# First transfers of an attention and MLP kernel in the order of their use, and a third group of queries, keys and values asked for earlier

## The chip, the cores and the metric

The kernel runs on one core of one Trainium2 chip. The metric is the device time of one execution in microseconds (us); lower is better. Engines are named as the profile names them: PE (TensorE, matrix products), DVE (VectorE), ACT (ScalarE), POOL (GpSimd), and SP (SyncE, which here only issues transfers).

## The reference, cut to what matters

```python
def _attn_ref(q, k, v) -> np.ndarray:          # q, k, v: (4, 8, 576, 64)
    window = 128
    scale = 1.0 / np.sqrt(D)
    scores = scale * np.matmul(q, k.transpose(0, 1, 3, 2))
    rel = pos[:, None] - pos[None, :]
    slopes = 2.0 ** (-8.0 * (np.arange(H, dtype=np.float32) + 1) / H)
    bias = slopes[:, None, None] * (-np.abs(rel).astype(np.float32))[None, :, :]
    mask = (rel >= 0) & (rel < window)
    scores = np.where(mask, scores + bias[None], -1000000000.0)
    scores = scores - np.max(scores, axis=-1, keepdims=True)
    attn = np.exp(scores)
    attn = attn / (np.sum(attn, axis=-1, keepdims=True) + 1e-09)
    return np.matmul(attn, v).astype(np.float32)
...
    x = attn_out.transpose(0, 2, 1, 3).reshape(B * S, H * D)     # 2304 x 512
    h = x @ w_in;  g = np.maximum(0.01 * h, h);  x = g @ w_out    # 512 -> 2048 -> 512
    h = x @ w_in2; g = h * (1.0 / (1.0 + np.exp(-1.702 * h))); out = g @ w_out2
```

Windowed attention with a linear bias per head, over four batches of eight heads, and then two MLP layers over all 2304 rows. Queries and keys are drawn with a larger spread than the values.

## The kernel before, in words

**Tiling.** A group n is four heads of one batch (two pairs of heads), so there are eight groups. `steps` holds 32 attention steps of 128 queries or so, four for each group. Steps 0 to 7 are batch 0, its groups 0 and 1 in turn; from step 8 on a group's four steps follow one another. The third group (n = 2) is thus used first by step 8. The keys of a group lie in `kbuf`, a part of the big tile `y` that also takes the result of the layers (`ys`); queries and values lie in pool buffers of two each, tags "q" and "v".

**A step.** `att_scores(s)` (L247) makes scores of queries by keys on PE. DVE adds the bias and takes the maximum (`att_ttr`, L265), ACT the exponential and its sum (`att_exp`, L277), DVE the reciprocal (`att_rcp`), POOL the division (`att_norm`). Two steps later PE transposes (`att_trans`, L296), ACT or DVE copy the result out of PSUM (`att_evac`, L304 and L306, tile `pt`), and three steps later PE multiplies by the values (`att_av`, L331, tile `O`). ACT and DVE split that into a high and a low part in `x` (L347, L127), since the layers take three passes over such parts.

**Weights.** A weight block comes as raw words (`load_w`, tile `raw`, two buffers) and `conv_w` makes its high and low part: ACT L142, DVE L143, L145, L147, L150 and L151, POOL L153, ACT L154, and a subtraction on POOL (L127). These nine operations are spread over thirteen ticks in the attention part, and in this part work in scratch `cearly`, eight regions of `y`. A raw buffer is free after L151, so that the load of conversion x + 2 waits for L151 of conversion x. `convs` is the table of steps at which conversions begin; each emits the load after next. From step 8 on a group of matmuls of the first layer (`mm1`, L367; `mm2`, L404) is put behind each step.

**Order.** All engines work through their instructions in the order written. SP issues nearly all loads in one queue, ACT some of the first. Both queues use eight semaphores for their transfers in turn, so that an issue also waits till the transfer eight before it has landed. `load_first` issues the loads of the first two groups and of two raw blocks; `load_qk(2, ...)` is called in step 6 and `load_v(2)` in step 9; the later groups are asked for at their predecessor's steps with i = 1 and i = 3.

Of the kernel before, what the change touches and what calls it, by code (L numbers as in the profile page):

```python
# [7 lines left out]
F32 = mybir.dt.float32  # L8
F32R = mybir.dt.float32r
U32 = mybir.dt.uint32  # L10
# [4 lines left out]
B, H, S, D = 4, 8, 576, 64  # L15
# [9 lines left out]
NKB = S // 64  # L25
# [6 lines left out]
def attention_mlp_kernel(  # L32
        ctx: ExitStack, tc: tile.TileContext, qin, kin, v, w1i, w1o, w2i, w2o, out):
    nc = tc.nc
# [5 lines left out]
    def sb(shape, dt, tag, bufs):  # L40
        return pool.tile(shape, dt, tag=tag, name=tag, bufs=bufs)
# [5 lines left out]
    window = [True]  # L47
# [3 lines left out]
    def after(d, fn):  # L51
        later.setdefault(step[0] + d, []).append(fn)

    def tick():
        step[0] += 1
        for fn in later.pop(step[0], []):
# [13 lines left out]
    ys = const.tile([128, NT * 4], F32, name="y")  # L70
# [5 lines left out]
    kbuf = ys[:, NT * 4 - 4 * S:].rearrange("p (n a s) -> p n a s", n=2, a=2)  # L76
    stile.append(ys[:, NT * 4 - 4 * S - 12 * 64:NT * 4 - 4 * S].rearrange(
        "p (n c h k) -> p n c h k", n=2, c=3, h=2))


    cearly = [[ys[:, x:x + 512].bitcast(U32) for x in (1536 + 1024 * n, 2048 + 1024 * n)]
              for n in range(4)] * 2

    def emit_consts():
        tmp = stile[2].rearrange("p n c h k -> p (n c h k)")
        rel, far = tmp[:, 0:KW], tmp[:, KW:2 * KW]
# [29 lines left out]
    def load_w(n, p):  # L116
        layer, f = divmod(n, NF)
        raw = sb([128, 1024], U32, "raw", 2)
        nc.sync.dma_start(out=raw, in_=wsrc[layer][p][f].bitcast(U32))
        wraw[n, p] = raw  # L120

    def alloc_w(n):
        wt[n] = wt[n - 2 * CB] if n >= 2 * CB else sb(
            [128, 4, 512], F32R, "wA" if n < CB else "wB", CB)

    def sub(e, out, in0, in1):
        e.tensor_tensor(out=out, in0=in0, in1=in1, op=ALU.subtract)  # L127

    def conv_w(n, p):
        raw = wraw.pop((n, p)).rearrange("p (n two) -> p n two", two=2)  # L130
        lo32, hi32 = raw[:, :, 0], raw[:, :, 1]
        if window[0]:
            a, b = cearly[4 * p + n]
        else:
            a = sb([128, 512], U32, "ca", 2)
            b = sb([128, 512], U32, "cb", 1)
        af, bf = a.bitcast(F32), b.bitcast(F32)
        hi, lo = wt[n][:, 2 * p], wt[n][:, 2 * p + 1]
        early = window[0]
        at = (0, 2, 3, 4, 5, 6, 7, 10, 12) if early else range(9)  # L140
        ops = [
            lambda: nc.scalar.activation(af, hi32.bitcast(F32), AF.Abs),  # L142
            lambda: nc.vector.tensor_scalar(  # L143
                af, af, F32_MIN_EXP, F32_MAX_EXP, op0=ALU.max, op1=ALU.min),
            lambda: nc.vector.tensor_scalar(  # L145
                a, a, 0x07FFFFFF, 3, op0=ALU.bitwise_and, op1=ALU.logical_shift_left),
            lambda: nc.vector.scalar_tensor_tensor(  # L147
                out=a, in0=hi32, scalar=0xC0000000, in1=a,
                op0=ALU.bitwise_and, op1=ALU.bitwise_or),
            lambda: nc.vector.tensor_scalar(b, a, 0xFF800000, None, op0=ALU.bitwise_and),  # L150
            lambda: nc.vector.scalar_tensor_tensor(  # L151
                out=bf, in0=lo32, scalar=2.0 ** -52, in1=bf, op0=ALU.mult, op1=ALU.mult),
            lambda: nc.gpsimd.tensor_tensor(out=af, in0=af, in1=bf, op=ALU.add),  # L153
            lambda: nc.scalar.activation(hi, af, AF.Copy),  # L154
            lambda: (sub(nc.gpsimd if early else nc.vector, lo, af, hi.bitcast(F32)),
                     ready.add((n, p))),
        ]
        for d, fn in zip(at, ops):
            after(d, fn) if d else fn()
# [9 lines left out]

    qkv, values = {}, {}  # L170

    def rows(src, offset, dims):
        return bass.AP(tensor=src.tensor, offset=src.offset + offset, ap=dims)


    def load_part(e, n, a, lo, hi):
        b, g = divmod(n, 2)
        qq, kk = qkv[b, g]
        src = qin[b, 2 * g + a]
        for h in range(2):  # L180
            d = slice(64 * h, 64 * h + 64)
            e.dma_start(  # L182
                out=qq[d, a, 64 * lo:64 * hi].rearrange("p (m q) -> p m q", q=64),
                in_=src[d].rearrange("p (m h q) -> p m h q", h=2, q=64)[:, lo:hi, h])
        e.dma_start(
            out=kk[:, a, 64 * lo:64 * hi], in_=kin[b, 2 * g + a, :, 64 * lo:64 * hi])

    def load_qk(n, parts=((0, NKB),)):
        b, g = divmod(n, 2)
        qkv[b, g] = sb([128, 2, S], F32, "q", 2), kbuf[:, n % 2]  # L190
        for lo, hi in parts:
            for a in range(2):
                load_part(nc.sync, n, a, lo, hi)

    def load_v(n, e=None):
        b, g = divmod(n, 2)
        vv = sb([128, 2, NKB, 64], F32, "v", 2)
        values[b, g] = vv

        for a in range(2):  # L200
            for h in range(2):
                for r in range(2):
                    src = v[b, 2 * g + a, 64 * r:64 * r + 64, 0:NQB - r, 64 * h:64 * h + 64]
                    k0 = 64 * (h ^ a)
                    (e or nc.sync).dma_start(out=vv[k0:k0 + 64, a, r::2], in_=src)  # L205

    def load_first():
        for n in range(2):  # L210
            qkv[0, n] = sb([128, 2, S], F32, "q", 2), kbuf[:, n]
        for n in range(2):
            for a, e in enumerate((nc.sync, nc.scalar)):
                load_part(e, n, a, 0, 4)
        load_w(*wload.pop())
        for a, e in enumerate((nc.sync, nc.scalar)):
            load_part(e, 0, a, 4, NKB)
        load_w(*wload.pop())
        load_v(0)
        for a in range(2):  # L220
            load_part(nc.sync, 1, a, 4, NKB)
        load_v(1)

    sp, sm, pp, pt, ot = {}, {}, {}, {}, {}
# [266 lines left out]
    wload = [(n, p) for p in range(2) for n in range(2 * CB)]  # L491
# [25 lines left out]
    for _ in range(6):  # L517
        nc.tensor.matmul(
            out=wp[:, 0:256], lhsT=wz[:, 0:128], rhs=wz[:, 128:384], start=True, stop=True)
    load_first()  # L520
    emit_consts()
    for n in range(2 * CB):
        alloc_w(n)
    convs = (0, 2, 3, 5, 6, 8, 10, 12)
    nconv, credit = 0, 0.0
    with tc.manual_schedule():
        for s in range(NS + 3):
            tick()
            todo, half = [], 0
            if s < NS:  # L530
                b, g, i = steps[s]
                nxt = 2 * b + g + 1 if b else 2 * B
                if nxt < 2 * B and i == 1:
                    load_qk(nxt)
                att_scores(s)
                if s == 6:
                    load_qk(2, ((0, 4), (4, NKB)))
                todo = items(s)
                half = len(todo) // 2
            if s >= 3:  # L540
                att_av(s - 3)
            if s < NS and nxt < 2 * B and i == 3:
                load_v(nxt)
            if s == 9:
                load_v(2)
            tr = 2 <= s < NS + 2
            if tr:
                for n in range(2):
                    att_trans(s - 2, n)
            for x, p in todo[:half]:  # L550
                att_ttr(s, x, p)
            if 1 <= s <= NS:
                att_rcp(s - 1)
                for x, p in items(s - 1):
                    att_norm(s - 1, x, p)
            for x, p in todo[:half]:
                att_exp(s, x, p)
            tick()
            if s >= 3:
                att_hi(s - 3)  # L560
            if tr:
                att_evac(s - 2, 0, nc.scalar)
            for x, p in todo[half:]:
                att_ttr(s, x, p)
            if tr:
                att_evac(s - 2, 1, nc.scalar if s < 9 else nc.vector)
            tick()
            for x, p in todo[half:]:
                att_exp(s, x, p)
            if s >= 3:  # L570
                att_lo(s - 3)
            tick()
            if s in convs:
                conv_w(*wconv[nconv])
                nconv += 1
                if nconv < 4 * CB - 1:
                    load_w(*wload.pop())
            seen = S * ((s - 2) // 8) if s != 8 and s != 9 else TT
            credit += 1
            while credit >= 1:  # L580
                j, fn, x = groups[-1]
                layer, c, t = rounds[j]
                need = [(layer * NF + c * CB + f, int(fn is mm2)) for f in range(CB)]
                if not ready.issuperset(need) or fn is mm1 and (t + 1) * TT > seen:
                    credit = 0
                    break
                credit -= 1
                run_group()
                tick()
        window[0] = False  # L590
        steady(wconv[4 * CB:])
# [47 lines left out]
```

## Time and profile before

| | us |
|---|---|
| three runs | 938.66, 938.48, 939.23; median 938.66 |
| profiled execution | 939.52 |
| its span | 937.5 |
| PE busy in the span | 903.6 (96%) |
| DVE, POOL, ACT busy in the span | 561.8, 390.7, 385.8 |

Busy times are those of the profiled execution. A matmul's end is modelled, so PE's busy share doesn't say how near to its peak it is. The span leaves out what lies around the program, 2.0 us here. "PEclk" is the granted clock of PE, 1.00 being its full 2.4 GHz and 0.50 half of it. The timeline's first number is the start in us from the span's begin, the second the time of the group of instructions.

### The profile page before, as it was taken

The page shows a single profiled execution, that of the slowest core. Times are in us where ns is not written, and L with a number is a line of the kernel's source. Part 1 is how long each engine was busy: PE and PEld are TensorE (multiplying, and loading weights), DVE is VectorE, ACT ScalarE, POOL GpSimd, SP SyncE. Part 2 cuts the span into 40 slices and gives each one's busy share as a digit, 9 for nine tenths or more (in the row PEclk, how much of TensorE's full clock was granted, in tenths as well). Part 3 has the DMA queues.
Part 4 walks back from the last instruction along what each step waited for, and adds up shares of the span by engine and source line. Part 5 has one row for each costly group of instructions (what it writes and reads, how often), then busy time and mean ns, then how long its engine had stood idle before and what let it go on. Part 6 is the DMA issues. An engine that isn't in the chain of part 4 may idle for free.

```text
span 937.5 us, 16388 instructions
## 1 busy us (share of the span) xinstructions
PE 903.6 (96%) x6252; PEld 844.6 (90%) x6252; DVE 561.8 (60%) x1220; ACT 385.8 (41%) x970; POOL 390.7 (42%) x448
## 2 busy tenths in 40 slices
PE   5678999999999999999999999999999999999997
PEld 3567998999999999999999998989989899898986
DVE  4876776137856473828375754657584848576343
ACT  3856887344423232323245455333232323233221
POOL 3765554224434242424349743433242423333221
PEclk7887999999999999999999999999999999999999
DMA  6363641002202020202011110202020201110034
GB/s 176 94 181 94 140 101 58 1 23 68 91 23 69 10 81 1 68 23 69 23 45 46 46 46 23 68 23 68 1 68 23 68 23 45 45 45 1 1 90 113
DMA packets 53934, 53.49 MB, mean 57 GB/s; under 512 B 40544, under 2 KB 42080, under 8 KB 53856
## 3 DMA queue, kind: packets, MB, share of 16 engines
q1 hardware_dynamic: 51664, 51.59, 19.4%
q10 hardware_dynamic: 2192, 0.85, 0.4%
q8 instruction: 50, 0.82, 0.4%
q14 instruction: 28, 0.23, 0.1%
HBM read 47.71 MB, written 4.72 MB: 56 GB/s over the span
## 4 chain that ended last, share of the span: by engine, by line
PE 92%; DMA 3%; SPq 2%; ACT 1%; DVE 1%; issue 1%; ACTq 0%; DVEq 0%
PE pt L367 20%; PE S L367 20%; PE mm L413 14%; PE mm L404 11%; PE O L404 10%; PE O L413 7%; PE O L331 2%; PE pt L296 2%; PE mm L367 2%; PE S L247 2%; DMA y<-k 1%; SPq L205 1%; DMA q<-q 1%; SPq L182 1%; ACT st L277 1%
## 5 line engine op out<-in xcount | busy, mean ns | idle before, releaser
L127 POOL TENSOR_TENSOR g<-u,g 128x384 fp32r<-128x384 f32 x192 | 202.1, 1053 | 437.4 <-ACT g L388 303.6
L388 ACT ACTIVATE g<-u 128x384 fp32r<-128x384 f32 x192 | 100.3, 522 | 47.3 <-DVE u L382 44.2
L424 DVE TENSOR_TENSOR y<-y,mm 128x384 f32<-128x384 f32 x88 | 48.5, 552 | 109.5 <-PE mm L404 80.1
L367 PE MATMUL pt<-x,wB 128*128 128x384 f32 x552 | 104.3, 337 | 0.0
L367 PE MATMUL pt<-x,wA 128*128 128x384 f32 x540 | 102.1, 337 | 0.0
L367 PE MATMUL S<-x,wA 128*128 128x384 f32 x540 | 101.9, 336 | 0.0
L367 PE MATMUL S<-x,wB 128*128 128x384 f32 x540 | 101.9, 336 | 0.0
L367 PEld LDWEIGHTS pt<-x,wB 128*128 128x128 f32 x552 | 97.9, 188 | 2.0
L367 PEld LDWEIGHTS S<-x,wB 128*128 128x128 f32 x540 | 95.5, 188 | 2.2
L367 PEld LDWEIGHTS S<-x,wA 128*128 128x128 f32 x540 | 95.5, 188 | 2.1
L367 PEld LDWEIGHTS pt<-x,wA 128*128 128x128 f32 x540 | 95.8, 188 | 1.8
L153 POOL TENSOR_TENSOR ca<-ca,cb 128x512 f32<-128x512 f32 x56 | 78.0, 1393 | 37.4 <-DVE cb L151 35.3
L378 ACT ACTIVATE u<-S 128x384 f32<-128x384 f32 x48 | 23.5, 490 | 132.6 <-PE S L367 132.6
L413 PE MATMUL mm<-wA,g 128*128 128x512 f32 x288 | 74.8, 395 | 0.0
L413 PE MATMUL mm<-wB,g 128*128 128x512 f32 x288 | 74.7, 395 | 0.0
L382 DVE SCALAR_TENSOR_TENSOR u<-u,pt 128x384 f32<-128x384 f32 x48 | 26.6, 554 | 70.7 <-ACT u L378 70.7
L429 DVE SCALAR_TENSOR_TENSOR y<-mm,y 128x512 f32<-128x512 f32 x84 | 57.8, 689 | 11.5 <-PE mm L413 11.5
L382 DVE SCALAR_TENSOR_TENSOR u<-u,S 128x384 f32<-128x384 f32 x48 | 26.6, 555 | 62.6 <-ACT u L378 62.6
L376 ACT ACTIVATE u<-S 128x384 f32<-128x384 f32 x42 | 20.6, 491 | 105.7 <-PE S L367 105.7
L404 PE MATMUL mm<-g,wA 128*128 128x384 f32 x312 | 64.0, 340 | 0.0
L404 PE MATMUL mm<-g,wB 128*128 128x384 f32 x312 | 63.6, 339 | 0.0
L413 PEld LDWEIGHTS mm<-wB,g 128*128 128x128 f32 x288 | 53.4, 188 | 9.2
(92 smaller groups left out, 1585.5 us busy)
## 6 DMA issues: line engine op xcount, KB each, us to landing
raw<-w1i SPq DMA_DIRECT2D x16, 512.0 KB, 3.6
raw<-w1o SPq DMA_DIRECT2D x16, 512.0 KB, 3.5
raw<-w2i SPq DMA_DIRECT2D x16, 512.0 KB, 3.5
raw<-w2o SPq DMA_DIRECT2D x16, 512.0 KB, 3.4
out<-y SPq DMA_DIRECT2D x36, 128.0 KB, 2.4
q<-q SPq DMA_DIRECT2D x20, 144.0 KB, 4.6
y<-k SPq DMA_DIRECT2D x10, 288.0 KB, 5.1
v<-v SPq DMA_DIRECT2D x32, 80.0 KB, 2.5
```

What stands on the lines that cost most here:

```text
L127: e.tensor_tensor(out=out, in0=in0, in1=in1, op=ALU.subtract)
L153: lambda: nc.gpsimd.tensor_tensor(out=af, in0=af, in1=bf, op=ALU.add),
L247: nc.tensor.matmul(out=sp[s][bank][64 * u:64 * u + 64, col:col + 64 * w], lhsT=qq[d, a, 64 * m:64 * m + 64], rhs=kk[d, a, k1 - 64 * w:k1], ...
L367: nc.tensor.matmul(out=h, lhsT=w[:, a, k * 128:(k + 1) * 128], rhs=xs[:, b2, k, t0:t0 + TT], start=(m == 0), stop=(m == len(ops) - 1),)
L376: nc.scalar.activation(u, h, AF.Prelu, alpha=0.01)
L378: nc.scalar.activation(u, h, AF.Tanh, scale=0.851)
L382: nc.vector.scalar_tensor_tensor(out=u, in0=u, scalar=1.0, in1=h, op0=ALU.add, op1=ALU.mult)
L388: nc.scalar.activation(g[:, 0], u, AF.Copy)
L404: nc.tensor.matmul(out=yp, lhsT=wt[n0 + f][:, 2 + a, e * 128:(e + 1) * 128], rhs=gt[r, f][:, b2, :], start=(m == 0), stop=(m == len(ops) - 1),
L413: nc.tensor.matmul(out=y, lhsT=gt[r, f][:, b2, e * 128:(e + 1) * 128], rhs=wt[n0 + f][:, 2 + a, :], start=(m == 0), stop=(m == len(ops) - 1),)
L424: nc.vector.tensor_tensor(out=acc, in0=acc, in1=y, op=ALU.add)
L429: nc.vector.scalar_tensor_tensor(out=acc, in0=y, scalar=0.5, in1=acc, op0=ALU.mult, op1=ALU.add)
```

## The change

Four things are changed.

- `load_first` issues in another order. `load_part` is split into `load_q` (queries of one pair) and `load_k` (the keys of both pairs in one transfer). The first raw block now stands behind the keys 4 to 8 of the first group, the second behind those of the second group. Four query transfers of the first group move from SP's queue to ACT's, and ACT issues no keys any more.
- The third group is asked for at step 4 (queries and keys) and step 5 (values), and lies in its own part of `y`, `late`. The groups behind it use the pool buffers as before.
- Conversions in the attention part no longer have eight scratch regions. They take the pool tiles `ca` (two buffers) and `cb` (one), of which every third `ca` and every second `cb` are replaced by a region of `y`.
- `convs` changes from (0, 2, 3, 5, 6, 8, 10, 12) to (0, 2, 4, 5, 7, 8, 10, 11).

```diff
--- before.py
+++ after.py
@@ -76,10 +76,6 @@
     kbuf = ys[:, NT * 4 - 4 * S:].rearrange("p (n a s) -> p n a s", n=2, a=2)
     stile.append(ys[:, NT * 4 - 4 * S - 12 * 64:NT * 4 - 4 * S].rearrange(
         "p (n c h k) -> p n c h k", n=2, c=3, h=2))
-
-
-    cearly = [[ys[:, x:x + 512].bitcast(U32) for x in (1536 + 1024 * n, 2048 + 1024 * n)]
-              for n in range(4)] * 2
     def emit_consts():
         tmp = stile[2].rearrange("p n c h k -> p (n c h k)")
@@ -129,11 +125,9 @@
     def conv_w(n, p):
         raw = wraw.pop((n, p)).rearrange("p (n two) -> p n two", two=2)
         lo32, hi32 = raw[:, :, 0], raw[:, :, 1]
-        if window[0]:
-            a, b = cearly[4 * p + n]
-        else:
-            a = sb([128, 512], U32, "ca", 2)
-            b = sb([128, 512], U32, "cb", 1)
+        x = 4 * p + n if window[0] else 0
+        a = ys[:, 1536:2048].bitcast(U32) if x % 3 == 2 else sb([128, 512], U32, "ca", 2)
+        b = ys[:, 2048:2560].bitcast(U32) if x % 2 == 1 else sb([128, 512], U32, "cb", 1)
         af, bf = a.bitcast(F32), b.bitcast(F32)
         hi, lo = wt[n][:, 2 * p], wt[n][:, 2 * p + 1]
         early = window[0]
@@ -169,32 +163,39 @@
     qkv, values = {}, {}
-    def rows(src, offset, dims):
-        return bass.AP(tensor=src.tensor, offset=src.offset + offset, ap=dims)
-
-
-    def load_part(e, n, a, lo, hi):
+
+    late = ys[:, 2560:2560 + 6 * S].rearrange("p (n a s) -> p n a s", n=3, a=2)
+
+    def new_qk(n):
+        qkv[divmod(n, 2)] = ((late[:, 0], late[:, 1]) if n == 2 else
+                             (sb([128, 2, S], F32, "q", 2), kbuf[:, n % 2]))
+
+
+    def load_q(e, n, a, lo, hi):
         b, g = divmod(n, 2)
-        qq, kk = qkv[b, g]
-        src = qin[b, 2 * g + a]
         for h in range(2):
             d = slice(64 * h, 64 * h + 64)
+            src = qin[b, 2 * g + a, d].rearrange("p (m h q) -> p m h q", h=2, q=64)
             e.dma_start(
-                out=qq[d, a, 64 * lo:64 * hi].rearrange("p (m q) -> p m q", q=64),
-                in_=src[d].rearrange("p (m h q) -> p m h q", h=2, q=64)[:, lo:hi, h])
-        e.dma_start(
-            out=kk[:, a, 64 * lo:64 * hi], in_=kin[b, 2 * g + a, :, 64 * lo:64 * hi])
-
-    def load_qk(n, parts=((0, NKB),)):
+                out=qkv[b, g][0][d, a, 64 * lo:64 * hi].rearrange("p (m q) -> p m q", q=64),
+                in_=src[:, lo:hi, h])
+
+    def load_k(n, lo, hi):
         b, g = divmod(n, 2)
-        qkv[b, g] = sb([128, 2, S], F32, "q", 2), kbuf[:, n % 2]
-        for lo, hi in parts:
-            for a in range(2):
-                load_part(nc.sync, n, a, lo, hi)
-
-    def load_v(n, e=None):
+        nc.sync.dma_start(
+            out=qkv[b, g][1][:, :, 64 * lo:64 * hi],
+            in_=kin[b, 2 * g:2 * g + 2, :, 64 * lo:64 * hi].rearrange("a p s -> p a s"))
+
+    def load_qk(n):
+        new_qk(n)
+        for a in range(2):
+            load_q(nc.sync, n, a, 0, NKB)
+        load_k(n, 0, NKB)
+
+    def load_v(n):
         b, g = divmod(n, 2)
-        vv = sb([128, 2, NKB, 64], F32, "v", 2)
+        vv = (late[:, 2].rearrange("p a (n d) -> p a n d", d=64) if n == 2 else
+              sb([128, 2, NKB, 64], F32, "v", 2))
         values[b, g] = vv
         for a in range(2):
@@ -202,23 +203,28 @@
                 for r in range(2):
                     src = v[b, 2 * g + a, 64 * r:64 * r + 64, 0:NQB - r, 64 * h:64 * h + 64]
                     k0 = 64 * (h ^ a)
-                    (e or nc.sync).dma_start(out=vv[k0:k0 + 64, a, r::2], in_=src)
+                    nc.sync.dma_start(out=vv[k0:k0 + 64, a, r::2], in_=src)
     def load_first():
         for n in range(2):
-            qkv[0, n] = sb([128, 2, S], F32, "q", 2), kbuf[:, n]
-        for n in range(2):
-            for a, e in enumerate((nc.sync, nc.scalar)):
-                load_part(e, n, a, 0, 4)
-        load_w(*wload.pop())
-        for a, e in enumerate((nc.sync, nc.scalar)):
-            load_part(e, 0, a, 4, NKB)
+            new_qk(n)
+        load_q(nc.sync, 0, 0, 0, 4)
+        load_q(nc.scalar, 0, 1, 0, 4)
+        load_k(0, 0, 4)
+        load_q(nc.scalar, 1, 0, 0, 4)
+        load_q(nc.sync, 1, 1, 0, 4)
+        load_k(1, 0, 4)
+        for a in range(2):
+            load_q(nc.scalar, 0, a, 4, NKB)
+        load_k(0, 4, NKB)
         load_w(*wload.pop())
         load_v(0)
         for a in range(2):
-            load_part(nc.sync, 1, a, 4, NKB)
+            load_q(nc.sync, 1, a, 4, NKB)
+        load_k(1, 4, NKB)
+        load_w(*wload.pop())
         load_v(1)
     sp, sm, pp, pt, ot = {}, {}, {}, {}, {}
@@ -521,7 +527,7 @@
     emit_consts()
     for n in range(2 * CB):
         alloc_w(n)
-    convs = (0, 2, 3, 5, 6, 8, 10, 12)
+    convs = (0, 2, 4, 5, 7, 8, 10, 11)
     nconv, credit = 0, 0.0
     with tc.manual_schedule():
         for s in range(NS + 3):
@@ -533,15 +539,15 @@
                 if nxt < 2 * B and i == 1:
                     load_qk(nxt)
                 att_scores(s)
-                if s == 6:
-                    load_qk(2, ((0, 4), (4, NKB)))
+                if s == 4:
+                    load_qk(2)
                 todo = items(s)
                 half = len(todo) // 2
             if s >= 3:
                 att_av(s - 3)
             if s < NS and nxt < 2 * B and i == 3:
                 load_v(nxt)
-            if s == 9:
+            if s == 5:
                 load_v(2)
             tr = 2 <= s < NS + 2
             if tr:
```

SP's queue at its start, before. `q`, `y` and `raw` are the targets of queries, keys and weights, `v` of values.

```order
L182 DMA q<-q 64x4x64 x2
L185 DMA y<-k 128x256
L182 DMA q<-q 64x4x64 x2
L185 DMA y<-k 128x256
L119 DMA raw<-w1i 128x1024
L182 DMA q<-q 64x5x64 x2
L185 DMA y<-k 128x320
L119 DMA raw<-w1i 128x1024
L205 DMA v<-v 64x5x64
```

SP's queue at its start, after.

```order
L179 DMA q<-q 64x4x64 x2
L185 DMA y<-k 128x2x256
L179 DMA q<-q 64x4x64 x2
L185 DMA y<-k 128x2x256
L185 DMA y<-k 128x2x320
L115 DMA raw<-w1i 128x1024
L206 DMA v<-v 64x5x64
```

The first raw block moved behind all keys of the first group, the second raw block behind the values and keys that follow, and the queries 4 to 8 of the first group left this queue.

SP's queue from the last value transfer of the second group on, before.

```order
L205 DMA v<-v 64x4x64
L119 DMA raw<-w1i 128x1024 x2
L119 DMA raw<-w1o 128x1024 x2
L182 DMA q<-q 64x4x64 x2
L185 DMA y<-k 128x256
L182 DMA q<-q 64x4x64 x2
L185 DMA y<-k 128x256
```

The same place after.

```order
L206 DMA v<-v 64x4x64
L115 DMA raw<-w1i 128x1024 x2
L179 DMA y<-q 64x9x64 x4
L185 DMA y<-k 128x2x576
L115 DMA raw<-w1o 128x1024
L206 DMA y<-v 64x5x64
L206 DMA y<-v 64x4x64
```

The queries and keys of the third group stand two raw blocks earlier, whole instead of in two parts, and its values follow one raw block behind them.

ACT's queue from step 3 to the third conversion, before. `st_67`, `st_68` are the score tiles of two steps, `sm` their sums.

```order
L277 ACTIVATE st_67,sm<-st_67,sm 128x3x64 x2
L142 ACTIVATE y<-raw 128x512
L277 ACTIVATE st_68,sm<-st_68,sm 128x64 x2
L277 ACTIVATE st_68,sm<-st_68,sm 128x2x64
L347 ACTIVATE x<-O 128x128 x2
L304 ACTIVATE pt<-pt 128x384 x2
```

The same place after.

```order
L283 ACTIVATE st_67,sm<-st_67,sm 128x3x64 x2
L283 ACTIVATE st_68,sm<-st_68,sm 128x64 x2
L283 ACTIVATE st_68,sm<-st_68,sm 128x2x64
L353 ACTIVATE x<-O 128x128 x2
L310 ACTIVATE pt<-pt 128x384 x2
L283 ACTIVATE st_68,sm<-st_68,sm 128x2x64
L283 ACTIVATE st_68,sm<-st_68,sm 128x3x64 x2
L136 ACTIVATE y<-raw 128x512
```

ACT's first operation of the third conversion, which reads a raw block, moved behind a whole step.

## Rows read from the trace of the kernel before

**Rows 1.** Windows of the span: us, busy (count) per engine, PEclk, DMA share, GB/s.

```profile
0.00:100.00 100.00, 71.49 (x980) 58.47 (x980) 67.13 (x273) 61.80 (x228) 60.22 (x105) 0.81 0.53 137
...
180.00:937.50 757.50, 752.19 (x4011) 712.44 (x4009) 448.30 (x716) 266.45 (x522) 291.31 (x258) 1.00 0.15 44
```

**Rows 2.** PE's waits in 0:100: in all, times, longest.

```profile
PE S L247 <- DMA y<-k: 12.1, 3, 6.7
PE mm L247 <- DMA y<-k: 4.9, 2, 3.7
PE O L331 <- DMA v<-v: 4.0, 4, 1.6
PE O L331 <- ACT pt L304: 3.8, 2, 2.3
```

**Rows 3.** Timeline of PE, start, us, operation, count [idle before].

```profile
23.08 0.92 PE L247 MATMUL mm<-y,q 64*64 64x192 f32 x8 [1.21 <-DMA y<-k]
...
33.36 1.08 PE L331 MATMUL O<-pt,v 64*64 64x128 f32 x32 [2.29 <-ACT pt L304]
...
50.63 0.92 PE L247 MATMUL S<-y,q 64*64 64x192 f32 x8 [6.67 <-DMA y<-k]
...
73.36 1.54 PE L331 MATMUL O<-pt,v 64*64 64x128 f32 x26 [1.13 <-DMA v<-v]
...
96.92 0.88 PE L247 MATMUL S<-y,q 64*64 64x192 f32 x16
```

**Rows 4.** Timeline of SP, issues.

```profile
11.74 5.18 SPq L205 DMA_DIRECT2D v<-v  x8
...
35.93 9.88 SPq L119 DMA_DIRECT2D raw<-w1o  x2
...
65.35 11.66 SPq L205 DMA_DIRECT2D v<-v  x16
```

**Rows 5.** Chain of waits in 0:100, transfers: start, us from issue to landing.

```profile
5.26 6.46 DMA q<-q
...
20.23 2.80 DMA y<-k
...
26.69 3.73 DMA raw<-w1i
...
56.28 4.02 DMA y<-k
```

**Rows 6.** Timeline of DVE, step 3's first reduce and conversion 1's last instruction.

```profile
24.14 0.36 DVE L265 CUSTOM_DVE_ANT_0 st<-mm,bias 128x192 f32<-128x192 f32 x1 [6.52 <-PE mm L247]
...
29.12 0.66 DVE L151 SCALAR_TENSOR_TENSOR y<-raw,y 128x512 f32<-128x512 uint32 x1
```

**Rows 7.** Windows: PE, PEld, DVE, ACT, POOL busy; PEclk, DMA share, GB/s.

```profile
24.10:97.00 72.90, 55.69 (x842) 46.86 (x838) 54.76 (x214) 50.08 (x186) 49.84 (x77) 0.83 0.46 123
31.20:49.30 18.10, 8.96 (x162) 6.66 (x162) 16.84 (x62) 14.98 (x60) 14.62 (x22) 0.88 0.30 93
...
80.70:97.00 16.30, 14.71 (x248) 12.94 (x244) 13.77 (x61) 12.84 (x51) 11.87 (x22) 0.90 0.31 82
...
38.10:48.40 10.30, 4.21 (x100) 3.09 (x92) 9.57 (x29) 8.22 (x31) 9.89 (x14) 1.00 0.24 79
48.40:55.20 6.80, 4.19 (x70) 3.40 (x71) 2.97 (x13) 1.82 (x7) 1.67 (x4) 0.50 0.68 170
72.30:79.10 6.80, 5.74 (x42) 5.62 (x43) 2.74 (x8) 2.20 (x9) 0.88 (x3) 0.50 0.49 113
```

**Rows 8.** Timelines of DVE and of POOL at one place.

```profile
39.27 1.30 DVE L143 TENSOR_SCALAR y<-y 128x512 f32<-128x512 f32 x1
...
39.02 1.27 POOL L127 TENSOR_TENSOR wA<-y,wA 128x512 fp32r<-128x512 f32 x1
```

**Rows 9.** Groups by line of DVE in 24.1:97.0: busy, mean ns, idle before.

```profile
L143 DVE TENSOR_SCALAR y<-y 128x512 f32<-128x512 f32 x7 | 6.5, 926 | 5.3 <-ACT y L142 5.3
...
L150 DVE TENSOR_SCALAR y<-y 128x512 uint32<-128x512 uint32 x7 | 5.1, 730 | 0.1
```


## The prediction

> **What bounds the kernel now.** I read the windows of the span first. In the first 100 us TensorE (PE) is busy 71.49 us at a mean granted clock of 0.81; in the last 757.5 us it is busy 752.19 at 1.00 [rows 1]. So some 28 us of idle PE, and the stretches of low clock, all lie in the first 100 us, where the attention of the first groups runs while weights are converted. The change touches nothing later, and I take the part from step 16 to the end (score matmul at 96.92 [rows 3]) as unchanged. The question is only how much earlier step 16 starts.
>
> Second, what PE waits for there: scores wait 12.1 and 4.9 us for keys, O matmuls 4.0 for values and 3.8 for ACT's copies of pt [rows 2]. Third, where: the PE timeline shows the large ones at step 3 (second half of its scores at 23.08), at the O matmul at 33.36 (2.29, behind ACT), at step 8 (50.63, wait 6.67, the first scores of the third group) and in the O matmuls of step 11 (the last piece at 73.36) [rows 3]. SP's queue shows why: the eight value loads of the first group leave SP between 11.74 and 16.92, the first 5.18 us behind the raw weights; at 35.93 two weight loads hold SP for 9.88 us, and the third group's keys stand behind them; the values of that group are issued from 65.35 on, behind another weight load [rows 4].
>
> **Step 3, first transfers.** What sets step 3 is the last piece of k(1), issued at 20.23, landed 2.80 us later at 23.03 [rows 5]. The old order puts two raw weights ahead of that; the new one puts one ahead, moves four query DMAs of the first group to ACT's queue and fuses the keys of two pairs. New SP order from the first raw: seven issues at about 0.65 us (5.18/8 [rows 4]) precede it, so it leaves at about 6. The program gives the DMAs eight semaphores in turn, each waits for the landing of the one eight before; the load that SP waits for in the trace (5.26 + 6.46, it lands at 11.72 [rows 5]) is a load behind the first raw. I expect the like: one of the last two v(0) issues waits till about 11.7. Then v, v, four q at 0.65 stand before the keys: 11.7 + 6 x 0.65 = 15.6. The fused transfer is twice the bytes of the old one (320 KB), so its duration is unknown: at least the 2.80 of the 160 KB piece, at most the 3.73 of a 512 KB raw [rows 5]. I take 3.3, landing at 19.0, against 23.03: 4.0 us earlier (range 3.5 to 4.5). The second raw is now issued behind it, at 16.3, and by the 3.73 lands at about 20; conversion 1 waits for it on ACT, ahead of step 3's exponentials. That is about when DVE has reduced step 3, so I cost it at nothing up to 1 us. Cover: DVE's first reduce of step 3 was at 24.14 [rows 6]; now about 20.2. ACT's queue had nine first issues (six of queries, three of keys) and now has eight, so its first exponential is not later; nothing.
>
> **What could be removed at most.** From step 3 on the removed waits are: 4.0 as above; 2.3 of the ACT wait for a raw at step 4 (33.36 [rows 3]; the raw issued at 26.69 landed 3.73 later [rows 5], and the new table converts at step 4 instead of 3); 6.67 at step 8; 4.0 for values at step 11 [rows 2, 3]; and the low clock behind the two long waits, half of 4.19 and of 5.74, 5.0 [rows 7]. The sum is 22.0. This is an upper bound, since it supposes that nothing else is late.
>
> **Third group.** Its keys are now asked for at step 4, behind the raw of conversion 3, which waits for the DVE instruction L151 of conversion 1 (at 29.12 [rows 6]). With step 4 some 3.5 earlier that is 25.6; then a raw and four query issues of 0.65 to 29. One pair's 288 KB of keys took 4.02 behind its queries [rows 5]; both pairs in one are 576 KB, at least 4.02, at most twice that, landing at 33 to 37. I take the lower part, since 512 KB of raw took 3.73. Step 8's scores would be ready to start at about 50.63 - 6.67 - 4.0 - 2.3 = 37.7. Margin 0.7 to 5 us, so I cost it at nothing. If that cover goes, the wait is some us at step 8, not the whole 6.67. The values, asked for at step 5, are needed three steps later still; nothing. The place in y is free there: y's first use by the layers is later in the program. The former eight scratch regions shrink to two pool buffers, one pool buffer and two regions of y. A conversion may thus wait for one two or three before it; with one conversion in one or two steps, these are done, so 0 to 1 us.
>
> **What is late next.** Without the DMA waits, DVE carries the stretch. Between 24.1 and 97.0 it is busy 54.76 of 72.9 us, ACT 50.08, POOL 49.84, PE 55.69 (part of it at half clock) [rows 7]. The DVE instructions between the first reduce of step 3 and step 16 are the same in the changed kernel: seven conversions, the reduces and the lower halves. No engine's work is smaller, so step 16 comes no earlier than DVE's work allows. How dense can it be? In 80.7:97.0, a stretch with no DMA wait, DVE is busy 13.77 of 16.30, 84%; in 31.2:49.3, 16.84 of 18.10, 93% [rows 7]. By the first: 54.76/0.84 = 65.2, step 16 at 20.2 + 65.2 = 85.4, a gain of 96.92 - 85.4 = 11.5. By the second: 58.9, step 16 at 79.1, gain 17.8. I take the first, because it is the only one of the two that holds MLP groups and attention steps together, as most of the new stretch will. So of the 22 us that PE's waits are worth about half comes out at the end.
>
> **The sum.** The profiled execution takes 939.52 against a span of 937.5; 2.0 lie around it and stay. 939.52 - 11.5 = 928.0 for an execution like the profiled one; the median of the runs is 938.66, so 927.1; I say 927.0.
>
> **Rivals.**
> 1. *Denser:* DVE at 93%: 938.66 - 17.8 = 920.9. For it: stretches of 15 us and more with such shares. Against: the first of them holds no MLP group, and steps there are ended by the chain reduce, exponential, norm, transpose.
> 2. *The cover gives back on the shared instructions.* L143 took 1.30 us at 39.27 while POOL's subtraction ran (39.02, 1.27) [rows 8]; means in the stretch are 0.926 for L143 and 0.730 for L150, seven each [rows 9]. If denser work put all of them beside a POOL instruction, at 1.30: 7 x (0.374 + 0.570) = 6.6 on the engine that bounds. Gain 11.5 - 6.6 = 4.9: 933.8. For it: POOL too is fuller when the same work takes fewer us. Against: such pairs already stand in the means. The Trainium skill, "SBUF — State Buffer", section "SBUF: two separate sides", says that DVE and GpSimd share a port pair as an exclusive lock, held for the whole instruction. By that rule this rival grows with density; the trace agrees with the lengthening at 39.27.
> 3. *It doesn't do what it says:* the third group still comes late, since its keys remain behind a raw that waits for a conversion; only step 3 gains, and 6.67 shrinks by little. Gain 1 to 4, 935 to 938. Against: the margin of 0.7 to 5 us.
> 4. *Slower: PE stays at half clock.* The stretch runs in short pieces on PE with gaps for DVE. PE was granted 0.83 on average over 24.1:97.0, so its 55.69 us are about 0.83 x 55.69 = 46.2 at full clock, an estimate. At half clock for a share f of it, it needs 46.2 x (1 + f). Slower than before starts where that exceeds 96.92 - 19.2 = 77.7, f = 0.68; at f = 1 it is 92.4, step 16 at 111.6, time 953. Against: 38.1:48.4 has PE busy 4.21 of 10.30 at clock 1.00, and the two long half-clock stretches, 48.4:55.2 and 72.3:79.1, come just behind the long waits that the change removes [rows 3, 7]. The Trainium skill, "TensorE: Matmul & The Clock Gate", section "A second HAM failure mode: psum-queue depth-cycling", tells of frequent small idle times that make the clock go up and down; by that rule the many short waits for DVE would hold it down. The trace speaks against it with the 4.21 of 10.30 at clock 1.00.
>
> **How the numbers follow.** Forecast (gain 9 to 15, around 927.0) 0.52; denser, 0.18; given back, 0.17; not doing what it says, 0.06; half clock, 0.07. The range of 8 in 10: the forecast's 923.7 to 929.7, most of the denser case (920.9, with a us beyond it for step 3) and most of the give-back case: 920.0 to 933.8, the rest of the chance lies outside. A measurement of this kernel tells 0.2%, 1.9 us, from no change. Faster: forecast, denser, give-back and half of the third, 0.90. Same: the rest of the third and a hundredth of the half clock, 0.04. Slower: 0.06.
>
> **What would show it.** Right: step 3's scores complete at about 19, no wait for keys or values on PE's O and S matmuls after step 3, step 8 at 38 to 41, step 16 at 82 to 88, DVE near 84% between step 3 and there, and the time from step 16 to the end as before. Wrong: a wait for y<-k on PE at step 8; L143 and L150 near 1.3 us on average; PE's clock at 0.5 over more than 25 us of the first 85; or the time behind step 16 longer, which my sum holds fixed.

## The result and the profile after

The changed kernel takes 926.04 us (median of 4 runs, 925.43 to 927.00) against 938.94 for the kernel before on the same chip: ratio 0.9860, 95% interval 0.9843 to 0.9877. The forecast was 927.0 in a range of 920.0 to 933.8. Its two main terms were each off by nearly 3 us, in opposite directions.

The profile after, windows first, columns as in [rows 1]. The third window is the stretch that the prediction summed: from DVE's first reduce of step 3 to step 16's scores.

```profile
0.00:100.00 100.00, 78.89 (x1231) 65.74 (x1232) 78.75 (x323) 70.77 (x268) 67.23 (x120) 0.88 0.61 149
...
180.00:925.20 745.20, 740.58 (x3944) 700.83 (x3943) 447.53 (x714) 262.46 (x512) 288.78 (x255) 1.00 0.15 45
...
22.90:85.30 62.40, 51.46 (x839) 42.93 (x832) 56.41 (x214) 49.99 (x186) 50.68 (x76) 0.92 0.61 146
```

PE is busy 78.89 of the first 100 us instead of 71.49, at a mean clock of 0.88 instead of 0.81. The stretch lasts 62.40 us; before it was 96.92 - 24.14 = 72.8. PE's waits in 0:100:

```profile
PE mm L253 <- DMA y<-k: 7.8, 2, 5.8
PE O L337 <- DVE x L123: 3.7, 4, 1.9
PE O L337 <- ACT pt L310: 2.6, 2, 1.4
...
PE S L253 <- DVE sm L271: 1.5, 2, 1.3
```

Against [rows 2] the waits of S for keys (12.1) and of O for values (4.0) are gone. What is left for keys, 7.8, is two waits, at steps 1 and 3. The waits of O for DVE's lower halves are 3.7 now; before they were 0.5. PE's timeline, the places of [rows 3]:

```profile
21.23 1.67 PE L253 MATMUL mm<-y,q 64*64 64x192 f32 x16 [5.75 <-DMA y<-k]
...
42.31 1.46 PE L253 MATMUL S<-y 64*64 64x192 f32 x16
...
61.03 1.08 PE L337 MATMUL O<-pt,y 64*64 64x128 f32 x32
...
85.30 0.88 PE L253 MATMUL S<-y,q 64*64 64x192 f32 x16
```

Step 3 (21.23) waits for its keys once, 5.75, and all sixteen matmuls follow; before, its second half began at 23.08. Step 8 (42.31, before 50.63) and step 11's O (61.03) wait for no transfer. Step 16 stands at 85.30 instead of 96.92, 11.6 earlier, and from there to the end it is 925.2 - 85.3 = 839.9 against 937.5 - 96.92 = 840.6. So the whole gain is made before step 16.

Why step 3 isn't earlier: the chain of waits, transfers from issue to landing, and SP's timeline.

```profile
2.48 3.97 DMA y<-k
6.47 6.26 DMA q<-q
12.73 0.02 issue
12.75 0.60 SPq L206
...
17.36 3.74 DMA y<-k
```

```profile
7.83 6.83 SPq L206 DMA_DIRECT2D v<-v  x8
14.71 2.61 SPq L179 DMA_DIRECT2D q<-q  x4
17.36 0.61 SPq L185 DMA_DIRECT2D y<-k  x1
...
32.85 0.69 SPq L185 DMA_DIRECT2D y<-k  x1
```

ACT issues a query transfer of the first group (its second pair, queries 4 to 8) at 6.47, and it lands at 12.73. SP's sixth value load must wait for it, by the eight semaphores used in turn. Then come two more value loads and four query loads at 0.65, and the keys leave at 17.36. This transfer stood in ACT's queue before too: of the four that the section on the change calls moved, only the two of the first pair came from SP. Before, it was issued at 5.26 and SP waited for it till 11.72 [rows 5]. Now its own issue has to wait, by the same semaphores, for the first fused keys, issued at 2.48 and landed at 6.45. The last row of SP's timeline is the issue of the third group's keys.

### The profile page after: what moved, and what is told of

Its sections match the earlier page's. It is cut to its first block, busy times and chain, and to the rows that moved or that the text cites. A ratio compares the mean times of both kernels' runs of the same rounds, so it can differ in the third digit from the quotient of the medians.

```text
span 925.2 us, 16379 instructions
## 1 busy us (share of the span) xinstructions
PE 899.4 (97%) x6252; PEld 841.6 (91%) x6252; DVE 564.0 (61%) x1220; ACT 386.7 (42%) x970; POOL 392.3 (42%) x448
## 3 DMA queue, kind: packets, MB, share of 16 engines
q1 hardware_dynamic: 50912, 51.85, 20.2%
## 4 chain that ended last, share of the span: by engine, by line
PE 93%; DVE 2%; DMA 2%; ACT 1%; SPq 1%; issue 0%; POOL 0%; DVEq 0%; POOLq 0%
PE pt L373 21%; PE S L373 20%; PE mm L419 15%; PE mm L410 12%; PE O L410 10%; PE O L419 7%; PE O L337 2%; PE pt L302 2%; PE S L253 2%; PE mm L373 2%; DMA y<-k 1%; DMA q<-q 1%; ACT st L283 0%; SPq L179 0%; DVE st L271 0%
## 5 line engine op out<-in xcount | busy, mean ns | idle before, releaser
L147 POOL TENSOR_TENSOR ca<-ca,cb 128x512 f32<-128x512 f32 x59 | 82.0, 1391 | 39.4 <-DVE cb L145 37.3
L435 DVE SCALAR_TENSOR_TENSOR y<-mm,y 128x512 f32<-128x512 f32 x84 | 57.8, 688 | 11.7 <-PE mm L419 11.7
```

The lines of the kernel that those rows point to most:

```text
L435: nc.vector.scalar_tensor_tensor(out=acc, in0=y, scalar=0.5, in1=acc, op0=ALU.mult, op1=ALU.add)
```

## Experiments

Ratios are to the kernel before, timed beside each kernel on the same chip; 0.001 is 0.94 us. Medians of different rows can come from different chips. Step times are starts of score matmuls in us, from one profiled execution each.

| kernel | median us | ratio (95%) | step 3 | step 8 | step 16 |
|---|---|---|---|---|---|
| before | 938.94 | 1 | 23.08, second half | 50.63 | 96.92 |
| changed | 926.04 | 0.9860 (0.9843 to 0.9877) | 21.23 | 42.31 | 85.30 |
| e1_first_order | 937.98 | 0.9980 (0.9969 to 0.9990) | 21.55 | 50.04 | 97.11 |
| e2_group_early | 930.31 | 0.9891 (0.9874 to 0.9908) | 22.88, second half | 47.23 | 88.69 |
| e3_old_table | 928.10 | 0.9873 (0.9859 to 0.9888) | 22.16 | 45.36 | 87.05 |
| e4_group_old_times | 935.88 | 0.9962 (0.9946 to 0.9978) | 21.35 | 51.54 | 94.65 |
| e5_more_dve | 976.38 | 1.0388 (1.0370 to 1.0406) | 20.80 | 53.44 | 129.31 |
| e5_more_act | 929.87 | 0.9889 (0.9872 to 0.9905) | 21.31 | 42.72 | 86.89 |
| e5_more_pool | 931.49 | 0.9906 (0.9891 to 0.9921) | 21.81 | 43.27 | 90.89 |
| e8_second_keys_first | 927.30 | 0.9860 (0.9845 to 0.9874) | 16.36 | 42.55 | 84.85 |
| e10_keys_and_table | 928.09 | 0.9871 (0.9854 to 0.9888) | 16.00 | 43.43 | 86.81 |
| e11_small_dve | 930.38 | 0.9898 (0.9883 to 0.9913) | 20.82 | 41.45 | 87.82 |
| e12_less_dve | 926.00 | 0.9851 (0.9828 to 0.9874) | 20.94 | 41.76 | 83.56 |
| e13_both | 926.58 | 0.9859 (0.9844 to 0.9873) | 16.23 | 42.21 | 84.66 |

**Which part carries the gain?** Four kernels that take the change apart.

e1: the kernel before with the changed `load_first`, `load_q` and `load_k`, nothing else.

```diff
-        for n in range(2):
-            for a, e in enumerate((nc.sync, nc.scalar)):
-                load_part(e, n, a, 0, 4)
+        load_q(nc.sync, 0, 0, 0, 4)
+        load_q(nc.scalar, 0, 1, 0, 4)
+        load_k(0, 0, 4)
...
```

> The kernel before with the new order of the first transfers alone (keys of two pairs in one there, later loads and the table as before). Theory 1 (DVE's work from step 3 to 16 sets the time, and what thinned it out was the late third group): the waits at steps 8 and 11 remain, step 3's first reduce comes about 1.2 us earlier as in the changed kernel, so 937 to 939. Theory 2 (the first transfers carry the gain, as the sum's 4.0 for step 3 had it): 3.5 us or more off, 934 to 935.5.

e2: the changed kernel with the old `load_first` and the old table.

```diff
-    convs = (0, 2, 4, 5, 7, 8, 10, 11)
+    convs = (0, 2, 3, 5, 6, 8, 10, 12)
...
+            for a, e in enumerate((nc.sync, nc.scalar)):
+                load_part(e, n, a, 0, 4)
```

> The changed kernel with the first transfers and the table of the kernel before: the third group early, with its place in y and the smaller scratch. Theory 1: it keeps 8 to 10 of the 12.5 us, 929 to 931, no wait for keys at step 8. Theory 2: 4 to 8, 931 to 935.

e3: the changed kernel with the old table alone.

```diff
-    convs = (0, 2, 4, 5, 7, 8, 10, 11)
+    convs = (0, 2, 3, 5, 6, 8, 10, 12)
```

> The changed kernel with the old table of conversion steps. Theory 1: the work on DVE is the same, so within 2 us of 926, 925 to 928; step 4 has ACT wait for a raw block. A rival (the table carries a part, since ACT waits for raw in the midst of step 4): 929 or more.

e4: the changed kernel with the third group asked for at the old steps.

```diff
-                if s == 4:
+                if s == 6:
                     load_qk(2)
...
-            if s == 5:
+            if s == 9:
                 load_v(2)
```

> The changed kernel with the third group asked for at the old steps (6 and 9), still in its place in y. Theory 1: the wait for keys at step 8 comes back for the most part, and the gain falls to 1 to 4 us, 935 to 938. Rival (the place in y frees the transfer of the next groups, and the early asking matters little): 927 to 931.

The score matmuls of step 8 on PE's timeline, in e1, e2, e3 and e4 in turn:

```profile
50.04 0.92 PE L267 MATMUL S<-y,q 64*64 64x192 f32 x8 [6.69 <-DMA y<-k]
```

```profile
47.23 0.88 PE L260 MATMUL S<-y 64*64 64x192 f32 x16 [2.43 <-DMA y<-k]
```

```profile
45.36 0.92 PE L253 MATMUL S<-y 64*64 64x192 f32 x8 [1.22 <-DMA y<-v]
```

```profile
51.54 1.56 PE L253 MATMUL S<-y 64*64 64x192 f32 x16 [9.51 <-DMA y<-k]
```

As to the times, e1, e2 and e4 fall where theory 1 had them, e3 (928.10) just above its 925 to 928; that e2 would have no wait for keys at step 8 was wrong. With the first transfers alone (e1) step 3 is 1.5 us earlier, but step 8 waits as long as before (6.69) and 0.2% is left at the end. The third group alone (e2) carries 1.09 of the 1.40%. With the group asked for late (e4) step 8 waits 9.51, and the gain falls to 0.38%. So the early asking does it, and the place in y without it doesn't; whether early asking would pay without that place was not run. e2 still waits 2.43 at step 8: with the old first transfers and table its keys come too late by that much. With the new first transfers (e3) 1.22 of a wait for transfers is left there, and with the new table nothing. e3's difference from the changed kernel, 0.0013, is within the two intervals; in its profile step 16 is 1.75 later.

**Is it DVE that sets the stretch then?** That is the other half of theory 1. Work that nobody waits for was added to one engine at a time, two instructions in each of steps 3 to 15 on a tile of its own. For e5_more_dve:

```diff
+    dose = const.tile([128, 384], F32, name="dose")
+    nc.gpsimd.memset(dose, 1.0)
...
+            if 3 <= s < 16:
+                for _ in range(2):
+                    nc.vector.reciprocal(dose, dose)
             if s in convs:
```

> The changed kernel with 26 more DVE instructions on a tile of their own (a reciprocal of 128x384, two in each of the steps 3 to 15), nobody waits for them. Each some 0.4 us, about 10 us more on DVE. Theory 1 (DVE's work sets the time from step 3 to 16): 80% or more of what they add comes out, 8 to 10 us, some 934 to 936. Rival (the chain of step to step sets it, DVE's 90% is a result): less than half, 927 to 931.

e5_more_act has `nc.scalar.activation(dose, dose, AF.Copy)` there:

```diff
-                    nc.vector.reciprocal(dose, dose)
+                    nc.scalar.activation(dose, dose, AF.Copy)
```

> The same with 26 more ACT instructions (a copy of 128x384, 0.4 us each, about 10 us). Theory 1: ACT is busy 80% of the stretch and has room of 12 us, so a third or less comes out, 927 to 930. Rival (chain): about as much as for DVE.

e5_more_pool has a multiplication by 1.0:

```diff
-                    nc.vector.reciprocal(dose, dose)
+                    nc.gpsimd.tensor_scalar(dose, dose, 1.0, 1.0, op0=ALU.mult, op1=ALU.mult)
```

> The same with 26 more POOL instructions (a multiplication of 128x384, about 0.9 us each, some 20 us). POOL is busy 81% of the stretch, with room for 12: theory 1: half or less of what they add comes out, 926 to 936. Rival (chain): most of it, 940 or more.

e11 has the reciprocal on 64 columns, since the large one came out far larger than meant:

```diff
-                    nc.vector.reciprocal(dose, dose)
+                    nc.vector.reciprocal(dose[:, 0:64], dose[:, 0:64])
```

> The changed kernel with 26 small reciprocals of 128x64 on DVE (two in each of steps 3 to 15). 2547 ns for 384 columns gives some 0.42 to 0.5 us each, 11 to 13 us in all, near the 13.6 us added to ACT (2.7 us came out) and the 15.9 added to POOL (4.3 came out). DVE sets the stretch: 70 to 90% comes out as it was with the large ones (50 of 66), ratio to before 0.994 to 0.998. Rival (the large ones only overran room that a small addition still finds): 20 to 30% as on ACT and POOL, 0.988 to 0.990.

The groups by line of the added work, of the four kernels in that order: total busy us, mean ns.

```profile
L583 DVE RECIPROCAL dose<-dose 128x384 f32<-128x384 f32 x26 | 66.2, 2547 | 0.4
```

```profile
L583 ACT ACTIVATE dose<-dose 128x384 f32<-128x384 f32 x26 | 13.6, 522 | 0.4
```

```profile
L583 POOL TENSOR_SCALAR dose<-dose 128x384 f32<-128x384 f32 x26 | 15.9, 612 | 1.1
```

```profile
L583 DVE RECIPROCAL dose<-dose 128x64 f32<-128x64 f32 x26 | 14.2, 547 | 0.4
```

What came out at the end, from the ratios against 0.9860: 66.2 us on DVE gave 49.6 (75%). 14.2 us on DVE gave 3.6 (25%), 13.6 on ACT 2.7 (20%), 15.9 on POOL 4.3 (27%); each of these three is uncertain by 2 us or so. So a small addition costs about the same on any of the three engines, within that uncertainty. The expected shares for ACT (a third or less) and POOL (half or less) came, but for 14.2 us on DVE theory 1 wanted 70 to 90%, and its rival 20 to 30%. So theory 1, by which DVE alone sets the stretch, falls for the kernel as it stands. The large dose by itself seemed to prove it, and the small one showed that it didn't.

The other direction, e12: the changed kernel with seven copies taken from DVE and given to ACT.

```diff
-                att_evac(s - 2, 1, nc.scalar if s < 9 else nc.vector)
+                att_evac(s - 2, 1, nc.scalar if s < 16 else nc.vector)
```

> The changed kernel with the second copy of pt on ACT instead of DVE up to step 15 (seven copies of 0.55 us less on DVE, seven of 0.4 more on ACT). DVE sets the stretch: 3.9 us off DVE less a fifth of 2.8 on ACT, 2 to 3.3 us faster than the changed kernel, ratio to before 0.983 to 0.984. Rival (chain): 0 to 1 us, 0.985 to 0.987, or slower.

Ratio 0.9851 against 0.9860, intervals lying over each other: not told apart, where theory 1 wanted 0.983 to 0.984. The windows from step 3's reduce to step 16, in e12, e11 and e5_more_dve in turn:

```profile
22.60:83.56 60.96, 50.48 (x840) 41.47 (x832) 50.99 (x207) 51.93 (x192) 52.59 (x76) 0.94 0.63 150
```

```profile
22.50:87.80 65.30, 52.44 (x838) 43.89 (x831) 64.00 (x236) 49.73 (x185) 49.64 (x75) 0.89 0.58 139
```

```profile
22.50:129.30 106.80, 67.21 (x838) 56.74 (x831) 105.83 (x234) 49.19 (x183) 48.68 (x74) 0.75 0.38 94
```

DVE's busy time (third figure) goes from 50.99 over 56.41 (changed kernel) to 64.00, and the stretch only from 60.96 over 62.40 to 65.30. At 64.00 of 65.30 DVE is all but full, and so it is in e5_more_dve with 105.83 of 106.80. From the one to the other the added work in the stretch grows by 48.0 us (24 reciprocals, 61.1 instead of 13.1) and the stretch by 41.5. So DVE becomes the bound at some 65 us; the changed kernel at 62.4 lies a little under that.

Why could a DVE that was 90% busy take 13 us more? In e11 its busy time without the added work fell from 56.41 to 50.9 (0.6 of that by two instructions outside the window) and its idle time from 6.0 to 1.3, so that only 2.9 of the 13.1 came out on the stretch. How that can fall shows in the groups by line of DVE in the stretch, first in the changed kernel, then in e5_more_dve (the lines are two higher there):

```profile
L290 DVE TENSOR_SCALAR sm<-sm 128x4 f32<-128x4 f32 (+1 forms) x13 | 6.9, 529 | 1.0 <-ACT st L283 1.0
...
L137 DVE TENSOR_SCALAR ca<-ca 128x512 f32<-128x512 f32 x5 | 4.1, 815 | 1.9 <-ACT ca L136 1.9
...
L139 DVE TENSOR_SCALAR ca<-ca 128x512 uint32<-128x512 uint32 x5 | 3.7, 740 | 0.0
```

```profile
L583 DVE RECIPROCAL dose<-dose 128x384 f32<-128x384 f32 x24 | 61.1, 2547 | 0.4
...
L292 DVE TENSOR_SCALAR sm<-sm 128x4 f32<-128x4 f32 (+1 forms) x13 | 4.1, 319 | 0.0
...
L141 DVE TENSOR_SCALAR ca<-ca 128x512 uint32<-128x512 uint32 x5 | 3.0, 601 | 0.0
...
L139 DVE TENSOR_SCALAR ca<-ca 128x512 f32<-128x512 f32 x5 | 2.0, 398 | 0.0
```

The same instructions take 529 or 319, 740 or 601, 815 or 398 ns. All of DVE's own work in the stretch of e5_more_dve is 105.83 less 61.1 of 24 added reciprocals, 44.7, against 56.41 in the changed kernel. Some 1.2 of that are four short instructions that fall outside the window there. So some 10.5 us of what the changed kernel's trace counts as busy are lengthening, not work. Two of the 128x4 instructions of the changed kernel, and POOL's instructions around them, tell where it comes from:

```profile
44.90 0.91 DVE L290 TENSOR_SCALAR sm<-sm 128x4 f32<-128x4 f32 x1 [0.33 <-ACT st L283]
...
53.27 0.16 DVE L290 TENSOR_SCALAR sm<-sm 128x4 f32<-128x4 f32 x1
```

```profile
44.50 1.28 POOL L147 TENSOR_TENSOR ca<-ca,y 128x512 f32<-128x512 f32 x1
...
51.15 1.36 POOL L123 TENSOR_TENSOR g<-u,g 128x384 fp32r<-128x384 f32 x1 [0.52 <-ACT g L394]
53.81 0.83 POOL L296 TENSOR_SCALAR y<-y,sm 128x192 f32<-128x192 f32 x2 [1.30 <-DVE sm L291]
```

The first begins while a TENSOR_TENSOR of POOL runs and ends 0.03 us behind that one's end; beside the second POOL is idle. So it is with all thirteen of this line: four begin with POOL idle and take 158 to 167 ns, nine begin beside a TENSOR_TENSOR of POOL, take 433 to 924 ns and end 0.02 to 0.03 us behind its end. In e5_more_dve, where POOL's work is spread over a longer time (48.68 of 106.80 against 50.68 of 62.40), ten take 164 to 168 ns and three 682 to 907. So for this line the cause is shown: it waits for POOL's instruction to end, and the trace counts the wait as busy. The Trainium skill, "SBUF — State Buffer", section "SBUF: two separate sides", states a port pair that GpSimd and some instructions of DVE (in a two-port mode, or with two inputs in SBUF) hold one at a time, for a whole instruction; the trace agrees with these ends. In which mode these instructions of DVE run, and how much of the 10.5 us the other lines lose in this way, was not measured.

**Can step 3 come earlier, and does it pay?** e8: in the changed kernel, the queries and keys of the second group go ahead of the first group's values.

```diff
         load_w(*wload.pop())
-        load_v(0)
         for a in range(2):
             load_q(nc.sync, 1, a, 4, NKB)
         load_k(1, 4, NKB)
+        load_v(0)
         load_w(*wload.pop())
```

> The changed kernel with queries 4 to 8 and the keys 4 to 8 of the second group ahead of the first group's values on SP. In the changed kernel those keys land at 21.1 and step 3 waits 5.75 us for them. Here they should land 3 to 5 us earlier, while the values are needed one matmul later. Theory 1: DVE begins step 3 earlier by 3 us and the end comes by as much, 922 to 924.5. Rival (step 3's O matmuls wait for the values and ACT for a raw block instead): 925 to 927.

e10: e8 with conversion 1 begun at step 3.

```diff
-    convs = (0, 2, 4, 5, 7, 8, 10, 11)
+    convs = (0, 3, 4, 5, 7, 8, 10, 11)
```

> e8_second_keys_first with conversion 1 begun in step 3 instead of 2. In e8 the keys came 5 us earlier, but DVE then waited 3.86 us for conversion 1, whose raw block lands at about 24. Behind step 3 that wait is covered: step 3's reduces and exponentials run through, and 2 to 4 us come out, ratio 0.982 to 0.984. Rival (conversion 1 is late itself: the weights are then late for the first layer group at step 8): 0.986 or more.

e13: e10 with the copies of e12.

```diff
-                att_evac(s - 2, 1, nc.scalar if s < 9 else nc.vector)
+                att_evac(s - 2, 1, nc.scalar if s < 16 else nc.vector)
```

> e10 with the copies of e12. If both gains are real and DVE sets the stretch they add up: 4 to 7 us below the changed kernel, ratio 0.978 to 0.982. If a chain or PE takes over, no better than the better of the two.

Step 3 came 4.9 us earlier in e8 and 5.2 in e10, and nothing of it reached step 8. DVE's timeline of e8, conversion 1:

```profile
24.68 0.43 DVE L137 TENSOR_SCALAR ca<-ca 128x512 f32<-128x512 f32 x1 [3.86 <-ACT ca L136]
```

and, from e10, PE's O matmuls of step 4 and the chain's transfer before them:

```profile
28.22 1.54 PE L337 MATMUL O<-pt,v 64*64 64x128 f32 x26 [0.99 <-DMA v<-v]
```

```profile
25.26 2.92 DMA v<-v
```

In e8 DVE waits 3.86 us for the raw block of conversion 1, which still stands behind keys and values: conversion 1 begins at 24.68, in the changed kernel at 24.50. With that out of the way (e10) the values of the second group, landing at 28.2, are the last. By 24.5 us SP has issued thirty transfers one by one at about 0.65 us; in both orders something that step 3 or 4 needs stands late in that queue. So both came out with their rivals, a few tenths of a us above the 925 to 927 in e8. e13 gives no more than the changed kernel. No version was found that is measurably faster than it.

## Why the prediction was right, point by point

- **Where it would happen.** Right: the part behind step 16 lasts 839.9 us against 840.6, and step 16 was forecast for 85.4 and came at 85.30.
- **Step 3, 4.0 us.** This term was too large, and so the sign "step 3's scores complete at about 19" failed. Measured: scores 1.85 us earlier (21.23 for 23.08), complete at 22.90, and DVE's first reduce 1.2 earlier (22.92 for 24.14 in [rows 6]), since now all sixteen matmuls must run before it (DVE's timeline; the second row is conversion 1, for the next point):

```profile
22.92 0.36 DVE L271 CUSTOM_DVE_ANT_0 st<-mm,bias 128x192 f32<-128x192 f32 x1 [5.13 <-PE mm L253]
...
24.50 0.64 DVE L137 TENSOR_SCALAR ca<-ca 128x512 f32<-128x512 f32 x1 [0.64 <-ACT ca L136]
```

  The step that failed in this term is SP's wait "till about 11.7", which I took over from the trace before, and with it the "nothing" for ACT's queue: I had counted its issues, and not that one of them waits for the fused keys. That put its landing, and SP's wait, at 12.73, 1.0 later. One issue more than I counted lay behind it (0.65), and the fused transfer took 3.74 instead of 3.3, as long as the dearer of my two bounds. The "5.18 us behind the raw weights" was misread: 5.18 is the time of the eight value issues together. The sum uses it only as such.
- **The second raw block, set to land "at about 20" and costed "at nothing up to 1 us".** It was issued at 18.01 instead of 16.3 and took 5.8 us instead of 3.73, so it landed at 23.8, and ACT waited 5.05 for it. DVE stood still for 0.64 of that, so the cost was in bounds while the landing was not:

```profile
23.79 0.68 ACT L136 ACTIVATE ca<-raw 128x512 f32<-128x512 f32 x1 [5.05 <-DMA raw<-w1i]
```

- **Third group.** Right that no wait remains and that about 6.67 goes with it. Its keys were issued at 32.85, 3.9 later than I had it, and took 6.5 us, so they landed at 39.3, outside my 33 to 37. Step 8 began at 42.31, 4.6 later than the 37.7 I set, so that the slips cancel and 3.0 us of cover are left; by my own 37.7 there would have been a wait. The 2.43 of e2 and the 1.22 of e3 show how thin the cover is.
- **What is late next.** The stretch was 62.40 us, not 65.2. By its own terms this is DVE at 56.41/62.40 = 90%, between my two ends of 84 and 93%, and 1.65 us more of DVE busy time than in [rows 7]. As a mechanism it is half right. "DVE carries the stretch" is the step that failed here. The measured sensitivity, 20 to 27% for each of three engines, shows that no engine alone sets the stretch at this length, and that a busy share of DVE is no measure of its work. What it is instead, presumably the round from scores over reduce, exponential and division to the transpose with each engine 80 to 90% filled, wasn't isolated; that stays open.
- **So the sum.** Start 2.7 later than set (22.92 for 20.2), stretch 2.8 shorter: 85.30 for 85.4. The number was right by the two errors cancelling, which is luck, and not because both terms held.
- **Rivals.** Denser: about half came (a stretch of 62.4 between 65.2 and 58.9). Give-back on DVE: 1.65 us instead of 6.6, and not on the two lines that I named: their means are 0.82 us (L137, before L143, 0.926) and 0.72 (L144, before L150, 0.730). Not doing what it says: e4 has that form, and gives 935.88, inside the 935 to 938 I set for it. Half clock: it didn't come; the mean granted clock of the stretch is 0.92 instead of 0.83, and PE's busy time there 51.46 instead of 55.69.

## What to carry to other kernels

Reordering the first loads moves a wait from one operand to another as long as one queue issues them at a fixed time each; count the issues ahead of each operand, and for every transfer on either queue also when it lands, since a later issue may wait for it by a shared semaphore. Asking for the third group ahead of the loads that wait for buffers was worth 9 to 10 of the 13 us here. To find what bounds a stretch, add a small amount to each engine in turn: a large dose can itself make the engine it is put on the bound, as 66 us on DVE did here, and then says nothing about the kernel as it stands.

## What the runs showed of the hardware that was not expected

- A reciprocal on DVE took 2547 ns for 128x384 and 547 ns for 128x64, 6.25 ns a column in between; I had expected 0.4 us for the large one. An ACT copy of the size of the large one took 522 ns.
- The same DVE TENSOR_SCALAR of 128x512 took 815 ns on average in the changed kernel and 398 ns with DVE overfull and POOL less dense. One of 128x4 took 158 to 167 ns with POOL idle, and up to 924 ns when it began beside a TENSOR_TENSOR of POOL, ending 0.02 to 0.03 us behind it; all of that counts as busy.
